# Two fused attention layers on one core: the first two pairs' row maxima from fp32 products, their sums copied by engines, a new list of steps

## The chip, the cores and the metric

One Trainium2 chip, one of its cores. The metric is the device time of one execution in microseconds (us): 652.89 us, the median of three runs (650.82 to 654.00). TensorE (PE) multiplies, VectorE (DVE), ScalarE (ACT) and GpSimd (POOL) do the rest, and SyncE (SP) issues the DMAs.

## The reference

A causal attention with a decaying bias, and behind it, on its output, a mixture of four attention heads. Batch 8, 576 positions.

```
# first layer: 8 heads of 64 columns
scores = scale * q @ k.T                      # causal
cum    = cumsum(max(s, 0))
scores = scores + min(-(cum[i] - cum[j]), 0)
attn   = softmax(scores);  x = attn @ v       # joined to [B, 576, 512]
# second layer: 4 experts of 64 columns, each with its own wq, wk, wv, wo
logits = x @ w_gate;  the 2 largest of 4, softmax over them = w
out   += w[e] * (softmax(causal(scale * (x wq[e]) (x wk[e]).T)) (x wv[e])) wo[e]
```

A softmax subtracts each row's maximum first. The kernel computes the causal bias as cum[j] - cum[i]; the second term is the same for a whole row and drops out, so a score is q·k plus the running sum at the key.

## The kernel before, in words

**Pairs and slots.** The work is cut into 48 pairs: two heads (or experts) of one batch, with the two heads side by side on the partitions. Pairs 0, 1, 2, ... are numbered in order, four first-layer pairs of a batch and then two second-layer pairs of the batch before it. A list written out by hand, `ORDER`, gives every step of the kernel as "slot:step"; the engines take their instructions from it in this order, each its own in its own queue, and wait on semaphores where a step needs another's result. Nothing else plans. Slot n holds the scores of pair n, the product with V of pair n-1, the maxima m3 to m5 of pair n+1 and m0 to m2 of pair n+2, the minus-maximum of pair n+1 and the preparation of later pairs. Slots -2 and -1 come before the first scores; so "-1:m3" is of pair 0 and "0:m3" of pair 1.

**A pair.** The scores stand keys by queries in PSUM, so that their exp goes into the product with V without a transpose. Because the maximum of a query's row then lies across partitions, it is found first from a second set of products, queries by keys: six PSUM banks (m0 to m5, `MBANKS`), 2,880 columns of each head, the left head on partitions 0 to 63 and the right one on 64 to 127, in bf16 (the upper half of each fp32 word, L729). VectorE reduces each bank with the mask to a column of `mcol` (M0 to M5, L744). TensorE turns mcol round (mt, L764), ScalarE copies it negated to 9 partitions (mA, L768) and two DMAs bring it into row 96 of the queries (mq, L773), where a row of ones on the key side adds it in the score products. Then s0 to s6 (products), E0 to E6 (exp, L819), b0 to b4 (causal selects on GpSimd), d0 to d5 (sums for the denominators, GpSimd), v0 to v8 (product with V), V0 and V1.

**Two kinds of pair.** Ordinary pairs hold q and k split into a high and a low fp32r part (h and l steps) and take two products for each score (L798, L803). Pairs 0 and 1 (`DIRECT`) are loaded into one tile, `plain`, as they are (h0 queries, h1 keys), and their scores are plain fp32 products (L792). Memsets fill rows 64 to 127 (z0 and z1 on VectorE, z2 and z3 on GpSimd).

**The running sum.** s is loaded (c0), made positive and scaled (c1, ScalarE), scanned (c2, VectorE, L457), and split into three parts by cuts and subtractions (c3, c4) in buffer `PB[1]`. For pairs 0 and 1 DMAs take the rest and the high part from there into rows 64 and 65 of the keys (hc, L632); for the others the three parts go to a DRAM tile `cum` (cu, L480) and from there to the keys (hc, L663).

**Fillers.** 60 spare products of 512 bf16 columns on a tile of zeros (i0 to i59, L1381) give TensorE something to do before the first scores: 40 ahead of the first maxima, 20 behind mt of pair 0. Eight PSUM banks are taken and given back in the list's order.

Of the kernel before, what the change touches and what calls it, by code (L numbers as in the profile page):

```python
# [8 lines left out]
F32 = mybir.dt.float32  # L9
F32R = mybir.dt.float32r  # L10
BF16 = mybir.dt.bfloat16
# [28 lines left out]
def pieces(kt, q0, q1):  # L40
# [22 lines left out]

ORDER = (
# [260 lines left out]
def order(pairs):  # L325
    for x in ORDER.split():
        n, step = x.split(":")
        yield int(n), step

COPY_Q, COPY_K = 3, 9
DIRECT = (0, 1)
SPARE = 60

FB = [0, 8, 10, 12]
NQK1 = 2
NQK2 = 3
RC = 96
RM = 96
# [1145 lines left out]
```

## Time and profile before

| | |
|---|---|
| median of three runs | 652.89 us |
| the profiled execution's own time | 653.66 us |
| its span, first to last instruction | 651.9 us |
| mean granted clock of TensorE, of 1.00 | 0.988 |
| TensorE busy | 639.9 us, 98% |
| VectorE, ScalarE, GpSimd busy | 514.0, 467.4, 414.4 us |

The span is 1.76 us shorter than the execution's time, which the profile doesn't show inside. TensorE's busy time is modelled (a product counts until its result is out, and products overlap), so 98% is not 98% of its peak. The granted clock is 1.00 at 2.4 GHz and 0.50 at 1.2 GHz.

### The profile page before, as it was taken

Reading aid. Unit: us, or ns where it says so; the run is one execution under the profiler, and the core shown is the slowest. Engines: PE = TensorE matmul, PEld = TensorE weight load, DVE = VectorE, ACT = ScalarE, POOL = GpSimd, SP = SyncE. Lnnn points to the kernel's source line nnn. Section 1 sums busy time; section 2 is a strip of 40 time slices with the busy share of each in tenths; the row PEclk is TensorE's granted clock in tenths of the full one; section 3 lists DMA queues with packets and bytes.
Section 4 is the critical chain, followed back from the end, with each engine's and each line's share of the span. In section 5 each row is a group of like instructions: output and inputs, shape, how many; then the busy total and the mean of one; then the engine's idle time right before and its main releaser. Section 6 shows DMA issues by size and latency. Waiting matters only on the chain.

```text
span 651.9 us, 16521 instructions
## 1 busy us (share of the span) xinstructions
PE 639.9 (98%) x5891; PEld 529.3 (81%) x5891; DVE 514.0 (79%) x1459; ACT 467.4 (72%) x1077; POOL 414.4 (64%) x558
## 2 busy tenths in 40 slices
PE   7999999999999999999999999999999999999997
PEld 3377798888887898888888888878987888889875
DVE  7587978996888768988778788888778867874894
ACT  5268978777768767777677767777587866576564
POOL 9298567676756585675594758638765669837030
PEclk9699999999999999999999999999999999999999
DMA  7433553452547446264464346553445725232313
GB/s 169 138 111 102 154 144 103 134 136 62 148 112 182 104 129 170 72 179 140 125 170 136 120 95 166 146 145 109 112 129 157 203 61 129 59 110 73 95 45 114
DMA packets 49559, 81.29 MB, mean 125 GB/s; under 512 B 19892, under 2 KB 19892, under 8 KB 49478
## 3 DMA queue, kind: packets, MB, share of 16 engines
q1 hardware_dynamic: 49478, 80.24, 46.4%
q8 instruction: 47, 0.77, 0.5%
q14 instruction: 34, 0.28, 0.1%
HBM read 44.61 MB, written 10.16 MB: 84 GB/s over the span
## 4 chain that ended last, share of the span: by engine, by line
PE 92%; DMA 3%; ACT 2%; DVE 1%; SPq 1%; issue 1%; ACTq 0%; DVEq 0%
PE pvp L908 20%; PE pq L1138 16%; PE s L798 11%; PE s L803 10%; PE mx L730 10%; PE pw L1138 9%; PE po L1138 7%; PE sm L961 4%; DMA raw<-in_qk_dram 2%; PE s L792 2%; PE i L1381 1%; PE s L839 1%; PE po L1112 1%; PE mt L764 1%; ACT p L819 1%
## 5 line engine op out<-in xcount | busy, mean ns | idle before, releaser
L744 DVE CUSTOM_DVE_ANT_0 sink<-mx,mask 128x64 bf16<-128x64 f32 (+7 forms) x432 | 169.5, 428 | 56.2 <-PE mx L730 41.4
L819 ACT ACTIVATE p<-s 128x512 f32<-128x512 f32 x288 | 160.4, 593 | 52.1 <-PE s L803 40.0
L851 POOL TENSOR_SCALAR_AFFINE_SELECT p<-p 128x256 f32<-128x256 f32 (+1 forms) x192 | 95.4, 506 | 142.0 <-ACT p L819 117.0
L798 PE MATMUL s<-q,k 128*128 128x320 f32 (+2 forms) x552 | 149.7, 297 | 0.0
L803 PE MATMUL s<-q,k 97*128 97x320 f32 (+2 forms) x552 | 141.4, 290 | 1.3 <-DMA q<-mr 1.3
L872 POOL TENSOR_TENSOR r<-r,p 128x640 f32<-128x640 f32 (+1 forms) x92 | 128.6, 1399 | 4.3
L798 PEld LDWEIGHTS s<-q,k 128*128 128x128 f32 x552 | 105.0, 190 | 7.8 <-issue 4.0
L803 PEld LDWEIGHTS s<-q,k 97*128 97x128 f32 x552 | 105.0, 190 | 2.2 <-DMA q<-mr 1.5
L1138 PE MATMUL pq<-x,wqkh 128*128 128x288 f32 x512 | 106.2, 300 | 0.0
L908 PE MATMUL pvp<-p,v 128*64 128x128 f32 (+3 forms) x1024 | 99.9, 321 | 0.0
L705 DVE TENSOR_TENSOR q<-raw,q 64x576 fp32r<-64x576 f32 x92 | 78.7, 870 | 25.2 <-ACT q L670 9.0
L711 DVE TENSOR_TENSOR k<-raw,k 64x1024 fp32r<-64x1024 f32 (+1 forms) x92 | 82.7, 913 | 13.7 <-PE s L798 6.0
L730 PE MATMUL mx<-k,q 96*64 96x512 bf16 (+7 forms) x920 | 86.3, 293 | 1.0 <-ACT p L844 1.0
L1138 PEld LDWEIGHTS pq<-x,wqkh 128*128 128x128 f32 x512 | 81.5, 188 | 2.5 <-ACT pv L922 1.0
L908 PEld LDWEIGHTS pvp<-p,v 128*64 128x64 f32 x1024 | 63.7, 136 | 23.3 <-issue 3.0
L1138 PE MATMUL pq<-x,wqkl 128*128 128x288 f32 x256 | 75.5, 295 | 0.0
L670 ACT ACTIVATE q<-raw 64x576 fp32r<-64x576 f32 x92 | 62.0, 678 | 6.3 <-DMA raw<-in_qk_dram 5.1
L674 ACT ACTIVATE k<-raw 64x128 fp32r<-64x128 f32 (+1 forms) x92 | 61.8, 680 | 5.2 <-DMA raw<-in_qk_dram 3.1
L730 PEld LDWEIGHTS <-q 96*64 96x64 bf16 x920 | 45.0, 110 | 19.7 <-issue 6.2
L867 POOL TENSOR_TENSOR r<-p 128x256 f32<-128x256 f32 x46 | 37.4, 812 | 34.1 <-ACT p L819 34.1
L869 POOL TENSOR_TENSOR r<-p 128x384 f32<-128x384 f32 x46 | 49.2, 1070 | 11.3 <-ACT p L819 11.2
L922 ACT ACTIVATE pv<-pvp 128x256 f32<-128x256 f32 (+1 forms) x92 | 36.5, 402 | 25.4 <-PE pvp L908 25.1
(146 smaller groups left out, 1162.8 us busy)
## 6 DMA issues: line engine op xcount, KB each, us to landing
raw<-in_qk_dram SPq DMA_DIRECT2D x30, 576.0 KB
rb<-rr SPq DMA_DIRECT2D x92, 144.0 KB
q<-q SPq DMA_DIRECT2D x45, 288.0 KB
k<-k SPq DMA_DIRECT2D x39, 288.0 KB
v<-in_vm_dram SPq DMA_DIRECT2D x32, 256.0 KB
out_dram<-o SPq DMA_DIRECT2D x32, 256.0 KB
q<-mr SPq DMA_DIRECT2D x92, 2.2 KB
plain<-in_qk_dram SPq DMA_DIRECT2D x4, 288.0 KB
```

Of the source, the lines that this page charges most:

```text
L670: nc.scalar.activation(q2[0:64, j], get_raw(n)[0:64, j], AF.Copy)
L705: nc.vector.tensor_tensor(a[64:128, j], get_raw(n)[0:64, j], q2[0:64, j].bitcast(F32), op=OP.subtract)
L711: nc.vector.tensor_tensor(part(c[0:64]), get_raw(n)[64:128, :, k], part(c[64:128]).bitcast(F32), op=OP.subtract)
L730: nc.tensor.matmul(t[64 * j : 64 * j + 64, c0 : c0 + k1 - k0], q2[0:RC, 64 * qt : 64 * qt + 64], keys(n, RC, j, k0, k1).bitcast(BF16)[:, 1 ...
L744: nc.vector.tensor_tensor_reduce(sink[:, c0 : c0 + w], t[:, c0 : c0 + w], mask[:, m0 : m0 + w], scale=1.0, scalar=mcol[n][:, 9:10] if bi = ...
L798: nc.tensor.matmul(t[0:nk, c0 : c0 + q1 - q0], K1[r1(n)][:, span(j, k0, k0 + nk)], Q1[r1(n)][:, j, q0:q1], start=True, stop=False,)
L803: nc.tensor.matmul(t[0:nk, c0 : c0 + q1 - q0], K2[r2(n)][0 : RM + 1, span(j, k0, k0 + nk)], Q2[r2(n)][0 : RM + 1, j, q0:q1], start=False, ...
L819: nc.scalar.activation(ptile[n][:, x % 2, 512 * ci : 512 * ci + 512], tl[x], AF.Exp, scale=0.125)
L851: nc.gpsimd.affine_select(out=a if kt else running()[:, :, 0:128], in_=a, pattern=[[64 if kt == 4 else 0, 2], [1, nk]], compare_op=OP.is_g ...
L872: add(r[:, :, q0:S], r[:, :, q0:S], p[:, :, 1024 + c : 1024 + c + S - q0], op=OP.add)
L908: nc.tensor.matmul(cur[h][64 * j : 64 * j + 64, q0 - PVC[h] : q1 - PVC[h]], vsl(j, kt), rtile[n][:, j, 0:128] if own else ptile[n][:, j, c ...
L1138: nc.tensor.matmul(t[0:nk, 0:w], l, r, start=(x == 0), stop=(x == len(terms) - 1))
```

## The change

For pairs 0 and 1 alone: (a) the products for the maxima are fp32, over all 128 rows, where they were bf16 over 96; (b) one row of keys carries the unsplit running sum, where two rows carried two parts of it; the scan now stands on partitions 64 to 127, and pair 0's two rows are copied by ScalarE (ha) and VectorE (hb), pair 1's are brought by two DMAs; (c) the split (c3, c4) and cu no longer stand ahead of these pairs; (d) the row of maxima is made by nine fp32 products, a column of mcol (128 rows by 1) with the identity, into three PSUM tiles of one partition (mt0: query tiles 0 to 3, mt1: 4 to 6, mt2: 7 and 8), and ScalarE writes each negated into row 96 (mA0 to mA2); the turn, the copy to 9 partitions and the two mq DMAs of these pairs go. (e) Sixteen spare products fewer: 24 ahead of the first maxima, 12 among the steps up to the first scores, 8 behind. (f) One memset of PB[1] waits for cu (lz). (g) The whole list of steps is new, to its end: of TensorE's steps about one in five keeps its successor.

In the diff below the list is cut after the steps of pair 1's scores.

```diff
+MROWS = [range(0, 4), range(4, 7), range(7, 9)]
...
 ORDER = (
+    "-2:z2 -2:i2 -2:i4 -1:z0 -1:z3 -2:id -2:f21 -2:f01 -2:i6 -2:i1 -2:i23 -2:i19 -2:i10 -2:f02 "
+    "-2:z1 -2:h1 -2:i3 -2:i18 -2:i12 -2:i7 -2:i13 -2:c0 -2:c1 -2:i0 -2:c2 -2:i5 -2:hb -2:i20 -2:ha "
+    "-2:i17 -1:z2 -2:h0 0:lv -1:ld 1:lk -2:i22 -2:i11 -2:z0 -1:z1 -2:i14 -2:i8 0:h2 0:ld 1:h1 "
+    "-2:i16 1:h2 1:h0 1:l3 2:lk -2:i15 -2:i21 -1:ha -2:i9 -2:z3 -2:m1 -2:m0 -1:m5 -2:ca -2:M1 "
+    "2:w0f -2:M0 -2:m2 -2:M2 5:w0f -1:h1 -1:m4 -2:f11 -1:m3 -1:M5 -1:mt1 1:l2 -1:mA1 -2:f20 -2:f10 "
+    "-2:i24 -2:lc -2:i25 2:w0h 2:l3 2:w0l 1:lq -2:i29 -1:mt0 -1:mA0 -2:i26 -2:i27 -2:i28 -1:M3 "
+    "-2:f22 -1:M4 -1:hb -1:h0 -1:m1 0:m5 -1:m2 0:m4 0:h3 -1:m0 1:ld 2:h2 2:h0 5:w0h 0:m3 -2:c3 "
+    "-2:c4 -2:cu 1:h3 -1:mt2 -2:i34 -2:i33 2:l0 2:lv -2:f12 -1:mA2 -2:i32 -2:i31 0:h1 2:l2 -2:i30 "
+    "-2:i35 -1:M1 0:s2 -1:M0 -1:M2 0:M5 0:s0 0:E2 0:M3 0:M4 0:E0 0:s4 0:E4 0:s5 0:E5 0:b2 0:s1 "
+    "0:b3 0:h0 1:l0 1:l1 0:s3 5:w0l -2:f00 0:E1 0:b0 0:b1 -2:i36 0:mt2 0:mA2 0:mt1 0:hc 1:m4 0:d0 "
+    "0:m0 1:s6 0:m2 0:m1 0:E3 2:l1 1:w0f 0:mA1 0:s6 1:m5 1:E6 1:m3 2:lq -2:lz -2:i39 0:E6 0:b4 "
+    "-2:i41 1:w0h -2:i38 -2:i40 -2:i37 -2:i43 -2:i42 1:M5 2:h1 1:M4 1:M3 3:w0f 3:w0h 2:ld 1:s3 "
+    "1:s5 2:hc 0:d1 0:d2 3:ld 0:d3 0:mt0 0:mA0 0:d4 0:d5 2:h3 1:E3 1:E5 1:s4 1:E4 1:b3 1:b4 1:s0 "
+    "1:b2 0:M2 0:M1 1:s2 0:M0 1:mt 1:s1 3:w0l 1:hc 1:E2 2:m5 3:m4 1:mA 1:v3 1:v5 2:m3 1:mq 1:v0 "
+    "1:m1 1:w0l 1:E1 2:M5 1:d2 1:E0 1:d1 1:b1 1:m0 1:M0 1:d3 1:d0 1:v4 1:v6 1:v1 1:v2 1:V0 1:lv "
...
-SPARE = 60
+SPARE = 44
...
-        for i in range(2):
-            for j in range(2):
-                nc.gpsimd.memset(PB[i][64 - 64 * j : 128 - 64 * j, j, PT:PCOLS], 0.0)
+        for i, j in ((0, 0), (0, 1), (1, 1)):
+            nc.gpsimd.memset(PB[i][64 - 64 * j : 128 - 64 * j, j, PT:PCOLS], 0.0)
         nc.gpsimd.memset(gwt, 0.0)
         nc.gpsimd.memset(tlt, 0.0)
         nc.gpsimd.memset(tgt, 0.0)
...
     def running_sums():
-        n = B * H
         t = {}
+        g = slice(64, P)

         def load_s():
             t["s"] = sb.tile([P, S], F32, tag="pv", name="s_t", bufs=5)
-            nc.sync.dma_start(t["s"][:n], s)
+            nc.sync.dma_start(t["s"][g], s.rearrange("(p j) s -> j p s", j=2))

         def positive():
             t["r"] = sb.tile([P, S], F32, tag="pv", name="s_r", bufs=5)
-            nc.scalar.activation(t["r"][:n], t["s"][:n], AF.Relu, scale=8.0)
+            nc.scalar.activation(t["r"][g], t["s"][g], AF.Relu, scale=8.0)

         def scan():
             t["c"] = sb.tile([P, S], F32, tag="pv", name="s_c", bufs=5)
-            r = t["r"][:n]
-            nc.vector.tensor_tensor_scan(t["c"][:n], r, r, 0.0, op0=OP.add, op1=OP.max)
+            early.append(t["c"])
+            r = t["r"][g]
+            nc.vector.tensor_tensor_scan(t["c"][g], r, r, 0.0, op0=OP.add, op1=OP.max)

         c4 = PB[1].rearrange("p a b -> p (a b)")[:, 0 : 4 * S].rearrange("p (t s) -> p t s", s=S)
-        early.append(c4)

         def cut(x, y):
             nc.vector.tensor_single_scalar(
-                y[:n].bitcast(I32), x[:n].bitcast(I32), -65536, op=OP.bitwise_and
+                y[g].bitcast(I32), x[g].bitcast(I32), -65536, op=OP.bitwise_and
             )

         def first():
             cut(t["c"], c4[:, 1])
-            nc.vector.tensor_tensor(c4[:n, 0], t["c"][:n], c4[:n, 1], op=OP.subtract)
+            nc.vector.tensor_tensor(c4[g, 0], t["c"][g], c4[g, 1], op=OP.subtract)

         def second():
             cut(c4[:, 0], c4[:, 2])
-            nc.vector.tensor_tensor(c4[:n, 3], c4[:n, 0], c4[:n, 2], op=OP.subtract)
-
-        return {"c0": load_s, "c1": positive, "c2": scan, "c3": first, "c4": second}
-
-    def keep_sums():
-        for j in range(2):
-            for k in (slice(0, 512), slice(512, S)):
-                nc.sync.dma_start(cum[:, :, span(j, k.start, k.stop)], early[0][j : B * H : 2, 1:4, k])
-
+            nc.vector.tensor_tensor(c4[g, 3], c4[g, 0], c4[g, 2], op=OP.subtract)
+
+        def keep_sums():
+            for j in range(2):
+                for k in (slice(0, 512), slice(512, S)):
+                    nc.sync.dma_start(
+                        cum[:, :, span(j, k.start, k.stop)], c4[64 + 32 * j : 96 + 32 * j, 1:4, k]
+                    )
+
+        return {"c0": load_s, "c1": positive, "c2": scan, "c3": first, "c4": second, "cu": keep_sums}

     def weights(name):
         w, hi, lo, n = {
...

-        def sums_in():
-            for j in range(2):
-                hd = 2 * i + j
-                nc.sync.dma_start(whole(n)[64:66, 2 + j], early[0][hd : hd + 1, 0:2])
-
-        items["hc"] = sums_in
+        def sums_in(j):
+            c = early[0][64 + 32 * j + n : 65 + 32 * j + n]
+            d = whole(n)[64:65, 2 + j]
+            if n:
+                nc.sync.dma_start(d, c)
+            elif j:
+                nc.vector.tensor_tensor(d, c, c, op=OP.max)
+            else:
+                nc.scalar.activation(d, c, AF.Copy)
+
+        items["ha"] = lambda: sums_in(0)
+        items["hb"] = lambda: sums_in(1)
         items["h0"] = lambda: nc.sync.dma_start(whole(n)[0:64, 0:2], heads[0:64])
         items["h1"] = lambda: nc.sync.dma_start(whole(n)[0:64, 2:4], heads[64:128])
         items["z0"] = lambda: nc.vector.memset(whole(n)[64:96, 0:2], 1.0)
...
         def sums_in():
-            if n < 2:
-                for j in range(2):
-                    hd = 2 * i + j
-                    for k in (slice(0, 512), slice(512, S)):
-                        nc.sync.dma_start(
-                            k2[64:67, span(j, k.start, k.stop)].bitcast(F32),
-                            early[0][hd : hd + 1, :, k],
-                        )
-            elif ph == 1:
+            if ph == 1:
                 nc.sync.dma_start(k2[64:67].bitcast(F32), cum[b * NP1 + i])
             else:
                 nc.sync.dma_start(k2[64:67].bitcast(F32), k2[67:70].bitcast(F32))
...
             mbank[n, bi] = t = take(f"mx{n}_{bi}")
             for qt, k0, k1, c0, _ in MBANKS[bi]:
                 for j in range(2):
-                    q2 = queries(n)[:, j].bitcast(BF16)[:, 1::2]
+                    if n in DIRECT:
+                        q, k = queries(n)[:, j], keys(n, P, j, k0, k1)
+                    else:
+                        q = queries(n)[0:RC, j].bitcast(BF16)[:, 1::2]
+                        k = keys(n, RC, j, k0, k1).bitcast(BF16)[:, 1::2]
                     nc.tensor.matmul(
-                        t[64 * j : 64 * j + 64, c0 : c0 + k1 - k0],
-                        q2[0:RC, 64 * qt : 64 * qt + 64],
-                        keys(n, RC, j, k0, k1).bitcast(BF16)[:, 1::2],
+                        t[64 * j : 64 * j + 64, c0 : c0 + k1 - k0], q[:, 64 * qt : 64 * qt + 64], k,
                         start=True, stop=True,
                     )

...
         t = {}
+
+        def row(x):
+            t[x] = take(f"mt{n}_{x}")
+            for y, qt in enumerate(MROWS[x]):
+                nc.tensor.matmul(
+                    t[x][0:1, 128 * y : 128 * y + 128], mcol[n][:, qt : qt + 1], ident,
+                    start=True, stop=True,
+                )
+
+        def copy_row(x):
+            a, w = MROWS[x][0], len(MROWS[x])
+            nc.scalar.activation(
+                queries(n)[RM : RM + 1].rearrange("p j (t c) -> p t j c", c=64)[:, a : a + w],
+                t[x][0:1, 0 : 128 * w].rearrange("p (t j c) -> p t j c", j=2, c=64),
+                AF.Copy, scale=-1.0,
+            )
+            give(t[x])
+
+        if n in DIRECT:
+            items = {}
+            for x in range(3):
+                items[f"mt{x}"] = lambda x=x: row(x)
+                items[f"mA{x}"] = lambda x=x: copy_row(x)
+            return items

         def turn():
             t[0] = take(f"mt{n}")
...
             steps.update(running_sums())
-            steps["cu"] = keep_sums
             steps["id"] = lambda: make_identity(nc, ident)
             steps["ca"] = causal
             steps["lc"] = late_constants
+            steps["lz"] = lambda: nc.gpsimd.memset(PB[1][64:128, 0, PT:PCOLS], 0.0)
             for i in range(NQK2):
                 for x, f in enumerate(fill(i)):
                     steps[f"f{i}{x}"] = f
```

## Rows read from the trace of the kernel before

**Rows 1.** Part 1 of the page: busy time of each engine over the span, its share, and instructions.

```profile
PE 639.9 (98%) x5891; PEld 529.3 (81%) x5891; DVE 514.0 (79%) x1459; ACT 467.4 (72%) x1077; POOL 414.4 (64%) x558
```

**Rows 2.** Busy time by stretch (us): PE, PE's weight loads, DVE, ACT, POOL, each with its number of instructions, then the granted TensorE clock, the DMA share and GB/s.

```profile
0.00:30.00 30.00, 24.62 (x102) 9.65 (x103) 18.23 (x39) 11.53 (x17) 18.58 (x37) 0.77 0.63 167
...
30.00:60.00 30.00, 28.69 (x255) 21.73 (x255) 26.03 (x90) 21.74 (x48) 24.62 (x32) 1.00 0.31 92
...
60.00:350.00 290.00, 290.00 (x2804) 245.59 (x2804) 235.68 (x679) 222.85 (x518) 196.09 (x255) 1.00 0.52 135
...
350.00:625.00 275.00, 273.98 (x2582) 235.94 (x2579) 216.39 (x624) 199.05 (x466) 171.98 (x227) 1.00 0.44 117
```

**Rows 3.** The chain of waits over the first 60 us: start, length, what.

```profile
16.33 3.05 PE mx L730 x22
...
25.01 5.00 PE i L1381 x13
...
30.00 5.49 PE s L792 x24
...
35.49 0.11 PE mt L764
...
54.33 3.92 DMA q<-mr
```

**Rows 4.** TensorE's spare products in order of time (start, length, line, tile, shape, count).

```profile
1.35 10.72 PE L1381 MATMUL i<-sink 128*128 128x512 bf16 x40 [1.35 <-DVE sink L373]
...
20.48 9.52 PE L1381 MATMUL i<-sink 128*128 128x512 bf16 x20
```

**Rows 5.** VectorE in order of time, first 46 us: a memset of the score operands, the running sum, one cut and one subtraction of it, and the first and the last reduction of a pair's maxima.

```profile
1.59 1.02 DVE L638 MEMSET plain<- 32x1152 f32 x1 [0.30 <-issue]
...
7.32 1.35 DVE L457 TENSOR_TENSOR_SCAN s_c<-s_r 64x576 f32<-64x576 f32 x1 [2.21 <-ACT s_r L452]
...
8.70 1.05 DVE L463 TENSOR_SCALAR p<-s_c 64x576 int32<-64x576 int32 x1
...
9.78 0.75 DVE L469 TENSOR_TENSOR p<-s_c,p 64x576 f32<-64x576 f32 x1
...
30.04 0.63 DVE L744 CUSTOM_DVE_ANT_0 sink<-mx,mask 128x448 bf16<-128x448 f32 x1 [4.72 <-PE i L1381]
...
34.38 0.08 DVE L744 DVE_READ_ACCUMULATOR2_ANT mcol<- 128x1 f32 x1
```

**Rows 6.** ScalarE in order of time, first 46 us; in brackets the idle time before and what ended it.

```profile
6.60 0.68 ACT L452 ACTIVATE s_r<-s_t 64x576 f32<-64x576 f32 x1
...
7.88 1.25 ACT L698 ACTIVATE k<-raw 64x1024 fp32r<-64x1024 f32 x2
...
12.26 0.31 ACT L674 ACTIVATE k<-raw 64x128 fp32r<-64x128 f32 x1 [3.13 <-DMA raw<-in_qk_dram]
...
31.03 0.60 ACT L819 ACTIVATE p<-s 128x512 f32<-128x512 f32 x1 [7.82 <-PE s L792]
...
38.10 0.38 ACT L922 ACTIVATE pv<-pvp 128x256 f32<-128x256 f32 x1 [1.37 <-PE pvp L908]
```

**Rows 7.** GpSimd in order of time, first 46 us: the causal mask (a memset, two selects) and the first select on a pair's exponentials.

```profile
9.49 0.77 POOL L376 MEMSET mask<- 128x576 bf16 x1
...
10.34 1.08 POOL L379 TENSOR_SCALAR_AFFINE_SELECT mask<-mask 64x64 bf16<-64x64 bf16 x2
...
32.63 0.77 POOL L851 TENSOR_SCALAR_AFFINE_SELECT p<-p 128x256 f32<-128x256 f32 x2 [12.53 <-ACT p L819]
```

**Rows 8.** SyncE's queue in order of time, first 46 us: start, time to issue, line, what, count.

```profile
2.62 1.26 SPq L635 DMA_DIRECT2D plain<-in_qk_dram  x2
...
14.61 2.52 SPq L480 DMA_DIRECT2D cum<-p  x4
```

**Rows 9.** DMA issues of the first 46 us: tile, source, queue, count, size.

```profile
raw<-in_qk_dram SPq DMA_DIRECT2D x5, 576.0 KB
...
plain<-in_qk_dram SPq DMA_DIRECT2D x4, 288.0 KB
...
w_qk<-in_wqk_dram SPq DMA_DIRECT2D x3, 256.0 KB
...
v<-in_vm_dram SPq DMA_DIRECT2D x3, 256.0 KB
...
s_t<-in_s_dram SPq DMA_DIRECT2D x1, 144.0 KB
```

**Rows 10.** Busy time by stretch, columns as in rows 2, around the fall and the rise of the granted clock.

```profile
5.00:10.00 5.00, 5.00 (x24) 2.23 (x23) 2.72 (x4) 3.17 (x5) 4.70 (x18) 1.00 1.04 204
...
15.00:16.00 1.00, 0.00 (x0) 0.00 (x0) 1.00 (x9) 0.99 (x2) 1.00 (x2) 0.75 0.59 194
...
29.00:30.00 1.00, 1.00 (x6) 0.33 (x4) 0.00 (x0) 0.00 (x0) 0.00 (x0) 0.93 0.48 138
```

**Rows 11.** The chain of waits over the whole span, its shares by line.

```profile
by line: PE pvp L908 19.7%; PE pq L1138 15.6%; PE s L798 10.8%; PE s L803 10.1%; PE mx L730 9.8%; PE pw L1138 8.5%; PE po L1138 6.5%; PE sm L961 3.8%; DMA raw<-in_qk_dram 1.8%; PE s L792 1.7%; PE i L1381 1.4%; PE s L839 1.3%; PE po L1112 1.
```

**Rows 12.** TensorE in order of time, 44 to 62 us: the product behind the one wait of this stretch.

```profile
58.30 0.42 PE L803 MATMUL s<-q,k 97*128 97x320 f32 x1 [1.31 <-DMA q<-mr]
```

**Rows 13.** TensorE's waits from 60 to 625 us, all of them: who waited, for what, us in total, times, the longest.

```profile
PE mx L730 <- ACT p L844: 1.0, 1, 1.0
```

497 rows, old and new, of the table ORDER are left out of this document.

## The prediction

> **What bounds the kernel now.** I read the page's busy shares first, then the stretches, then the chain of waits for the start, then each engine's own order there. TensorE is busy 98% of the span, VectorE 79%, ScalarE 72% [rows 1]. From 60 to 625 us TensorE is busy in every microsecond but one, at a granted clock of 1.00 [rows 2], and that one is its only wait there, 1.0 us [rows 13]. So in this stretch the time is TensorE's work, and no order of steps shortens it by more than that microsecond. What can move lies ahead of 60 us.
>
> The first 30 us hold little work. 40 spare products run from 1.35 us for 10.72 us, then come the maxima of pairs 0 and 1 in bf16, then 20 more spare products from 20.48 us for 9.52 us [rows 4], and the first score product at 30.00 us [rows 3]. The clock falls at about 15.5 us, in a microsecond in which TensorE does nothing, and is back in the microsecond before the first scores [rows 10]; the mean of the 30 us is 0.77 [rows 2]. From 30 to 60 us TensorE loses 1.31 us [rows 2], all in one wait for a maxima row of a later pair, whose DMA took 3.92 us [rows 3, 12].
>
> **The maxima's cost.** The trace has no fp32 product for maxima, so it is bounded. Below: as now; 22 of the 40 products for two pairs took 3.05 us at half clock [rows 3], so 20 at full clock take 1.4 us. Above: the fp32 score products of pair 0, 24 records for 12 products and 3,072 columns, took 5.49 us [rows 3], 1.79 ns a column; 5,760 columns would take 10.3 us. Nearest is the product with V, fp32 like them, with two heads in the two halves of the columns: 19.7% of 651.9 us [rows 11] for 48 pairs is 2.68 us a pair, for 1,600 columns of each head. That is half the price of the score products, so the two halves run side by side, and 2,880 columns take 4.8 us. I take 4.8.
>
> **The products with the identity.** 128 columns at 1.79 ns are 0.23 us; nine make 2.1 us a pair. Below, as today's turn, 0.11 us in all [rows 3].
> This price is where a page speaks against the change: the Trainium skill, "TensorE: Matmul & The Clock Gate", Terms, has trn2's transpose mode four times faster for fp32. The row's 0.11 us times four would be 0.44 us a product, by estimate 4.0 us a pair in place of 2.1; my time would rise by 3.8 us. No run here shows it.
>
> **The start, step by step.**
> - s: today 576 KB go ahead of it [rows 9] and its relu starts at 6.60 us [rows 6]. Now 288 KB of keys do; 288 KB less at 204 GB/s [rows 10] is 1.4 us, so 5.2 us. Relu 0.68 [rows 6], scan 1.35 [rows 5]: 7.25 us. The copy on VectorE is priced as a subtraction of that width, 0.75, the memset behind it 1.02 [rows 5]: 9.0 us. GpSimd needs seven memsets of that size and the identity first, to about 8.9 us. TensorE's 24 spare products, at 10.72/40 us each [rows 4], end at 7.8 us. First product at 9.1 us.
> - Pair 0: 4.8 us, to 13.9. The causal mask on GpSimd, 0.77 and 1.08 us [rows 7], stands behind that last memset, so VectorE reduces from 10.8 us; six banks take 4.4 us [rows 5], and what mt1 needs is there at 13.2. mt1 0.7, three spare products at 0.21 (24 in 5 us [rows 10]), mt0 0.9, three more: 16.8 us.
> - Pair 1's last load. Ahead of it and with it go four loads of `plain` and s, two raw, one of v and two of weights, 3.25 MB [rows 9]. Today ScalarE gets the raw of pair 2 at 12.26 us [rows 6], with 2.16 MB issued up to it; the other 1.09 MB at 204 GB/s take 5.3 us: 17.6 us. TensorE waits 0.8 us. Pair 1's products end at 22.4, mt2 at 22.9. ScalarE's copy of two query tiles costs 0.38, as a copy of 256 columns [rows 6], beside six spare products, 1.25 us. First score at 24.1 us, not 30.0: 5.9 us earlier.
> - The steps taken out on SyncE's queue (mq, and the hc DMAs) free it; cu, 2.52 us of issue [rows 8], moves behind c4. On VectorE c3 and c4, two of 1.05 and two of 0.75 us at most [rows 5], move behind pair 0's reductions. The last two of these stand behind preparations: ScalarE has the raw of pair 3 at 12.3 us (again 2.16 MB issued up to it), 3.7 us of copies on it (one of keys is 1.25 us for its two parts [rows 6]), a row copy and a weight copy to 17.0; then VectorE takes the weights' low part, 0.75, and the two reductions, 1.5: 19.2 us. Behind c3 and c4 wait pair 1's reductions, whose first freed bank the third score chunk needs: 19.2 + 3.6 + two preparations of 0.75 + 0.8 is 25.1 us, against 25.9 when TensorE comes to it. That cover is 0.8 us thick. Pair 2's maxima need cu and then hc: 22.8 + 2.52 + two landings, about 29 us, against 31 when they are due.
> - Added behind the first score: eight spare products, 1.7 us; pair 1's nine products with the identity, 2.1; less two turns, 0.2. Scores and the rest are as today. 3.6 us of the 5.9 are given back: 2.3 us left.
> - The row copies, up to 0.60 us for 512 columns [rows 6], are off the path: they lie beside spare products or scores.
>
> **From there to 60 us.** exp starts 5.9 us earlier, and with it GpSimd, whose first select now comes at 32.63 us after 12.53 us idle [rows 7]. The maxima row that comes late at 58.30 us hangs on this chain, so I take its 1.31 us as gone. If it stays, that is the second rival.
>
> **The rest.** After 60 us I take nothing: bounds -1.0 (the one wait goes) and +3 (a few new waits of the kind at 58.30 us). Sum: 2.3 + 1.3 = 3.6 us. 653.66 - 3.6 = 650.1 us against the profiled execution; the median lies 0.77 us below that execution, so 649.3 us.
>
> **The rivals.**
> 1. The clock (slower). If it falls during the fp32 maxima and stays at 0.50 as long as today, 13.5 us (15.5 to 29), TensorE does 6.75 us of work less in that time, and unlike today that is real work. 649.3 + 6.75 = 656. Place: from 9 to 24 us; it decides if the waits at 7.8 to 9.1 and 16.8 to 17.6 us grow to the 1.86 us that TensorE stood still before 16.33 us today. For it: today's fall, and sixteen fillers fewer. Against: between the two waits it would be busy without a break, which today it was not. Chance 0.14.
>  The same page of the Trainium skill, Part 1: The HAM clock gate, has the half clock as the default and activity as what releases it; the trace agrees (it falls in the idle microsecond and is back at 0.93 in the last one of the second row of spare products, by rows 4 and 10).
> 2. The start's gain is given back by 60 us: VectorE is busy 26.0 of the 30 us from 30 to 60, more than its share later [rows 2], and pairs 2 to 4 may wait for their rows as pair 3 does today. What is left is 0 to 1.5 us: 651.4 to 653. Chance 0.23.
> 3. The new list makes TensorE wait anew in the steady part, three waits like that of 58.30 us: +4, 653.3 us. For it: most neighbours are new. Against: TensorE has other work in its queue at each. Chance 0.06.
> 4. The change does not do what it says: the two halves do not run side by side in fp32 here. 10.3 in place of 4.8 us, twice: +11, 660 us. Against it is the product with V. Chance 0.03.
> 5. More than forecast: loads land earlier, fp32 maxima start at 8 us, and the steady wait goes: 646. Chance 0.12.
>
> **How the numbers follow.** The forecast, 648 to 651.4 us, has 0.42. What a measurement can tell from no change is 0.5%, 3.26 us, so the bounds are 649.6 and 656.2. Faster: 0.12 and, as 649.3 lies at the edge, 0.26 of the 0.42, in all 0.38. Slower: 0.07 (half of rival 1), 0.03 and 0.02 of rival 3: 0.12. The rest, 0.50, is same. Range 645.5 to 655.5: it leaves out rival 4, half of rival 1 and the far part of rivals 3 and 5.
>
> **What would show it.** Right: first fp32 maxima at 8.5 to 10 us; a pair's six banks on TensorE in about 5 us; nine products with the identity at 0.2 us each; the granted clock at 1.00 from 5 us on; the first score at 24 us; pair 1's scores done some 2 us before today's; no wait at 50 to 60 us; 60 to 625 us as dense as now. Wrong: 0.50 in any microsecond between 9 and 30; ten microseconds for a pair's maxima; a first score after 27 us; more than 2 us of waits after 60 us.

## The result, and the profile after

The changed kernel takes 660.95 us, the median of four runs (659.58 to 663.51), the kernel before 652.42 us beside it: a ratio of 1.0136 (95% interval 1.0110 to 1.0161), 8.5 us slower. The forecast was 649.3 us, the range 645.5 to 655.5: wrong, and on the wrong side. The profiled execution, the slowest of the four, took 663.51 us, with a span of 661.8 us, 9.9 us more than the 651.9 of before.

The chain of waits of the changed kernel from 0 to 62 us (start, length, what), cut after the first scores, which answers to [rows 3]:

```profile
1.65 8.64 DMA s_t<-in_s_dram
10.32 0.69 ACT s_r L454
11.03 1.36 DVE s_c L460
12.47 2.21 DMA plain<-s_c
14.68 0.15 issue
14.82 6.64 PE mx L735 x40
21.47 0.75 PE mt L768 x6
22.22 0.75 PE i L1408 x3
22.97 0.96 PE mt L768 x8
23.93 0.76 PE i L1408 x3
24.69 5.01 PE mx L735 x40
29.70 0.53 PE mt L768 x4
30.23 0.34 PE i L1408
30.61 0.39 PE i L1408
31.04 1.02 PE i L1408 x4
32.06 5.29 PE s L819 x24
```

The first line is the news. The load of s, 144 KB, is issued nearly first and takes 8.64 us; before, with 576 KB ahead of it, its relu (the step that makes s positive) started at 6.60 us [rows 6]. Everything up to the first product hangs on it. ScalarE's own lines up to the relu, VectorE's memset behind the scan and the copy of pair 0's sums, and TensorE's lines of pair 0's maxima and first scores (start, length; in brackets the idle time before and what ended it):

```profile
0.81 1.28 ACT L454 ACT_TABLE_LOAD   x1 [0.81 <-PEq L1500]
10.32 0.68 ACT L454 ACTIVATE s_r<-s_t 64x576 f32<-64x576 f32 x1 [8.23 <-DMA s_t<-in_s_dram]
```
```profile
13.44 1.02 DVE L646 MEMSET plain<- 32x1152 f32 x1 [0.19 <-issue]
```
```profile
14.82 6.64 PE L735 MATMUL mx<-plain 128*64 128x384 f32 x40 [6.65 <-DMA plain<-s_c]
31.90 5.45 PE L819 MATMUL s<-plain 128*128 128x320 f32 x24
```

The chain and TensorE's line put the wait's end down to a DMA of `plain`, which is pair 1's row. More likely it is the memset, which ends at 14.46 us: in the three kernels `after`, `a_two` and `a_first` pair 0's products start 0.36 us behind the end of that memset (14.82, 11.53 and 12.91 us), while the trace names three different releasers. By either way they hang on the scan, and so on s.

TensorE stands still for 6.65 us, and the clock falls under it. Windows of one microsecond (from:to, then busy of PE, PEld, DVE, ACT, POOL, the granted clock, DMA share, GB/s):

```profile
10.00:11.00 1.00, 0.00 (x0) 0.00 (x0) 0.00 (x0) 0.68 (x1) 1.00 (x2) 1.00 0.90 331
11.00:12.00 1.00, 0.00 (x0) 0.00 (x0) 0.97 (x1) 0.00 (x0) 1.00 (x2) 0.60 0.15 55
...
17.00:18.00 1.00, 1.00 (x4) 0.26 (x2) 0.73 (x4) 0.99 (x2) 0.73 (x1) 0.50 1.12 207
18.00:19.00 1.00, 1.00 (x18) 0.71 (x16) 0.62 (x3) 0.64 (x2) 0.00 (x0) 0.99 0.93 183
```

So pair 0's products run at 1.2 GHz up to 18 us and take 6.64 us; pair 1's, the same forty records at 2.4 GHz, take 5.01. The later stretches, as in [rows 2], and TensorE's waits from 60 to 625 us (total, times, longest), against 1.0 us in [rows 13]:

```profile
30.00:60.00 30.00, 29.83 (x237) 20.62 (x236) 22.07 (x80) 20.32 (x43) 22.08 (x31) 1.00 0.41 114
60.00:350.00 290.00, 288.70 (x2806) 245.65 (x2803) 234.76 (x679) 224.61 (x514) 200.81 (x256) 1.00 0.50 133
350.00:625.00 275.00, 273.05 (x2561) 230.95 (x2560) 213.77 (x611) 195.38 (x460) 173.14 (x226) 1.00 0.45 119
```
```profile
PE s L830 <- DMA q<-mr: 1.9, 2, 1.3
PE s L825 <- ACT pv L949: 0.4, 1, 0.4
PE pvp L935 <- POOL r L892: 0.4, 1, 0.4
PE pq L1165 <- DVE x L1067: 0.2, 1, 0.2
```

How far the changed kernel lies behind at four points of the two traces (first scores are given here and below by TensorE's own line, where that of before starts at 29.89; the chain of [rows 3] has 30.00):

| | before | after | behind by |
|---|---|---|---|
| first score product | 29.89 | 31.90 | 2.0 us |
| turn of pair 2's maxima | 41.92 | 47.68 | 5.8 us |
| turn of the last pair's maxima | 615.25 | 624.05 | 8.8 us |
| end of the span | 651.9 | 661.8 | 9.9 us |

Over half of the loss is there by 48 us; the steady part adds 3.0, of which 1.9 is waits (2.9 against 1.0), and the end 1.1. The split between these last two is rough: a pair's turn stands at another place in the new list, and from pair to pair the turns of the changed kernel lie 3.6 to 10.6 us behind those of before.

### The profile page after: what moved, and what is told of

Same layout as the page of the kernel before. It is cut to its first block, busy times and chain, and to the rows that moved or that the text cites. A ratio compares the mean times of both kernels' runs of the same rounds, so it can differ in the third digit from the quotient of the medians.

```text
span 661.8 us, 16686 instructions
## 1 busy us (share of the span) xinstructions
PE 645.9 (98%) x5949; PEld 532.2 (80%) x5949; DVE 511.6 (77%) x1460; ACT 472.2 (71%) x1082; POOL 418.2 (63%) x558
## 4 chain that ended last, share of the span: by engine, by line
PE 90%; DMA 5%; DVE 2%; SPq 1%; ACT 1%; issue 1%; POOL 0%; ACTq 0%; DVEq 0%
PE pvp L935 19%; PE pq L1165 15%; PE s L825 11%; PE mx L735 11%; PE s L830 10%; PE pw L1165 8%; PE po L1165 6%; PE sm L988 4%; PE s L819 2%; DMA s_t<-in_s_dram 1%; PE s L866 1%; DMA q<-q 1%; PE po L1139 1%; PE mt L791 1%; PE i L1408 1%; DVE sink L747 1%
## 5 line engine op out<-in xcount | busy, mean ns | idle before, releaser
L878 POOL TENSOR_SCALAR_AFFINE_SELECT p<-p 128x256 f32<-128x256 f32 (+1 forms) x192 | 93.4, 495 | 149.5 <-ACT p L846 137.3
L825 PE MATMUL s<-q,k 128*128 128x192 f32 (+2 forms) x552 | 151.3, 299 | 0.7 <-ACT pv L949 0.4
L830 PE MATMUL s<-q,k 97*128 97x192 f32 (+2 forms) x552 | 141.5, 291 | 1.9 <-DMA q<-mr 1.9
L899 POOL TENSOR_TENSOR r<-r,p 128x640 f32<-128x640 f32 x92 | 130.0, 1413 | 5.3
L712 DVE TENSOR_TENSOR k<-raw,k 64x1024 fp32r<-64x1024 f32 (+1 forms) x92 | 81.3, 894 | 15.9 <-DMA k<-k 9.7
L735 PE MATMUL mx<-k,q 96*64 96x256 bf16 (+7 forms) x920 | 87.9, 293 | 0.0
L896 POOL TENSOR_TENSOR r<-p 128x384 f32<-128x384 f32 x46 | 52.0, 1131 | 12.4 <-ACT p L846 12.4
L1054 DVE TENSOR_TENSOR pv<-pv,rb 128x576 f32<-128x576 f32 x46 | 43.5, 948 | 10.3 <-DMA rb<-rr 9.7
```

What stands on the lines that cost most here:

```text
L712: nc.vector.tensor_tensor(part(c[0:64]), get_raw(n)[64:128, :, k], part(c[64:128]).bitcast(F32), op=OP.subtract)
L735: nc.tensor.matmul(t[64 * j : 64 * j + 64, c0 : c0 + k1 - k0], q[:, 64 * qt : 64 * qt + 64], k, start=True, stop=True,)
L825: nc.tensor.matmul(t[0:nk, c0 : c0 + q1 - q0], K1[r1(n)][:, span(j, k0, k0 + nk)], Q1[r1(n)][:, j, q0:q1], start=True, stop=False,)
L830: nc.tensor.matmul(t[0:nk, c0 : c0 + q1 - q0], K2[r2(n)][0 : RM + 1, span(j, k0, k0 + nk)], Q2[r2(n)][0 : RM + 1, j, q0:q1], start=False, ...
L878: nc.gpsimd.affine_select(out=a if kt else running()[:, :, 0:128], in_=a, pattern=[[64 if kt == 4 else 0, 2], [1, nk]], compare_op=OP.is_g ...
L899: add(r[:, :, q0:S], r[:, :, q0:S], p[:, :, 1024 + c : 1024 + c + S - q0], op=OP.add)
```

## The experiments

Unless said otherwise, a time is a median beside runs of the kernel before on the same chip (651.5 to 652.0 us), and a first score is that of the profiled execution.

**The load of s.** In the changed kernel one DMA reads s as two halves of 32 rows, `(p j) s -> j p s`, so that its first dimension counts 2. In `a_two` the same bytes go to the same partitions in two DMAs of 32 rows:

```diff
-            nc.sync.dma_start(t["s"][g], s.rearrange("(p j) s -> j p s", j=2))
+            for j in range(2):
+                nc.sync.dma_start(
+                    t["s"][64 + 32 * j : 96 + 32 * j], s.rearrange("(p j) s -> j p s", j=2)[j]
+                )
```

> The changed kernel, s loaded by two DMAs of 32 rows each in place of one with two dimensions. Theory A (the one load of s is slow by its form, two outer entries that only few DMA engines serve): relu of s begins at 5.0 to 6.6 us in place of 10.32, the first maxima product at 9 to 11 us in place of 14.82, the clock stays at 1.00, the first score at about 26 us; the time falls by 5 to 7 us, to about 655 us. Theory B (s is late because v and two raw loads issued behind it share the engines): relu still at 9 to 10.5 us, the time within 1 us of the changed kernel.

656.75 us, ratio 1.0082 (1.0045 to 1.0120). In its trace:

```profile
5.73 1.28 ACT L457 ACT_TABLE_LOAD   x1 [5.73 <-DMA s_t<-in_s_dram]
7.03 0.68 ACT L457 ACTIVATE s_r<-s_t 64x576 f32<-64x576 f32 x1
```
```profile
11.53 5.08 PE L738 MATMUL mx<-plain 128*64 128x384 f32 x40 [2.18 <-DMA raw<-in_qk_dram]
27.05 5.45 PE L822 MATMUL s<-plain 128*128 128x320 f32 x24
```

The relu is 3.3 us earlier, TensorE waits 2.18 us in place of 6.65, the clock stays at 1.00, the products take 5.08 us and the first score comes 4.85 us earlier: 4.2 us of the 8.5 are gone. The load itself gains more than the relu does. By the semaphore records of the traces s has landed at 5.66 us, 4.6 us earlier; the relu then waits for ScalarE's `ACT_TABLE_LOAD` of 1.28 us, which stands behind the wait for s here, and in the changed kernel ran at 0.81 us, long before s. All eight kernels here with s in two DMAs have it there, at 5.40 to 5.73 us; no run moves it, and what it costs in the end was not tried.

`a_first` leaves the load as the change has it and puts the DMA of pair 1's first row (`-1:ha`), which waits for the scan, ahead of the loads of v and raw on SyncE's queue:

```diff
-... -2:h0 0:lv -1:ld ... 2:lk -2:i15 -2:i21 -1:ha
+... -2:h0 -1:ha 0:lv -1:ld ... 2:lk -2:i15 -2:i21
```

> The changed kernel with its one load of s; the DMA of pair 1's first row of sums stands in SyncE's queue right behind the load of pair 0's queries, so that v and both raw loads are issued only after the scan. Theory A: with the engines to itself the load still needs several us on few engines, relu at 7 to 9 us. Theory B: relu at 5 to 6 us. The time by either is unsure by 3 us, since the raw loads now come later; the relu's start is what tells.

662.12 us, 1.0161 (1.0139 to 1.0184). The relu starts at 8.34 us: with little behind it in the queues the load is 2.0 us quicker, and still its landing is 2.7 us later than that of the two loads of `a_two` with all the others behind them (8.32 against 5.66). What was held back lands late, so that pair 1's maxima and the first score (33.6 us) come later.

`b_form` puts the form of the load alone into the kernel before (the rows are picked accordingly behind it):

```diff
-            nc.sync.dma_start(t["s"][:n], s)
+            nc.sync.dma_start(t["s"][:n], s.rearrange("(p j) s -> j p s", j=2))
```

> The kernel before, with the changed kernel's form of the load of s (one DMA, two outer dimensions, heads in the order even then odd; the rows are picked accordingly behind it). Theory A: relu at 9.5 to 12 us in place of 6.60, the first maxima 3 to 5 us later; the time rises by 2 to 5 us since twenty spare products behind the maxima hide nothing of it. Theory B: relu at 6.6 us as before, same time.

657.0 us, 1.0076 (1.0048 to 1.0104), and in its trace

```profile
11.32 0.69 ACT s_r L452
...
32.80 5.49 PE s L793 x24
```

the relu is 4.7 us later than in [rows 6] and the first score 2.8 us later than before. By the medians the access pattern costs 4.2 us in one kernel and 5.1 in the other. The 5.1 holds more than the load: the profiled execution is the fastest of `b_form`'s four (654.69 us, span 1.1 us longer than before), and the other three, 656.8 to 658.8 us, ran at a lower mean clock (0.985 to 0.987 against its 0.989). That `a_first`'s load was 2.0 us quicker says that loads issued behind it slow it too; it holds them back in turn: of pair 0's queries, issued behind it, 14 of the sixteen increments of the semaphore have come by 7.06 us in the changed kernel, the last two at 10.09 and 10.88, where in `a_two` all have come by 7.10.

**The fp32 maxima.** `b_fp32` is the kernel before with fp32 products for pairs 0 and 1 (two memsets moved forward for it), nothing else; `a_two_bf16` is `a_two` with bf16 ones.

```diff
-                    q2 = queries(n)[:, j].bitcast(BF16)[:, 1::2]
+                    if n in DIRECT:
+                        q, k = queries(n)[:, j], keys(n, P, j, k0, k1)
```

> The kernel before with the maxima of pairs 0 and 1 as fp32 products over 128 rows and nothing else of the change (two memsets of the score operands stand earlier, so that all rows are filled). At 5.0 us a pair at full clock in place of 1.3 to 1.5 the first score comes 4 to 7 us later if the clock stays up, 10 or more if it falls as it does before; the time rises by that much. If the wait for the maxima row, and not TensorE, held the first scores, the time rises by under 2 us.

652.88 us, 1.0016 (0.9995 to 1.0038): no difference. Ten microseconds of products (12.65 to 22.9) stand where the idle time and half-clock fillers were, and the clock stays up:

```profile
0.00:30.00 30.00, 27.31 (x142) 13.41 (x143) 18.13 (x40) 11.55 (x17) 18.29 (x37) 1.00 0.57 143
```

against 24.62 us at 0.77 in [rows 2]. The price of the products and the clock that they keep up cancel here. One of the 23 runs of the kernel before beside `b_fp32` kept its clock by itself: mean 1.000, a span of 644.5 us, where the median is 650.2 and `b_fp32` has 649.6 to 651.6 at 0.999 to 1.000. There is no trace of that run, but by it fp32 maxima do cost some 6 us at the same clock.

> As the first of these runs (s in two DMAs), and the maxima of pairs 0 and 1 from bf16 products again, 96 rows, on the one row of sums. The maxima are then rounded, which a softmax cancels. If fp32 products cost what the page's shares gave (4.8 us a pair against 1.4), this is faster than the first run by up to 6.8 us less what pair 1's loads then leave waiting: first score at 22 to 24 us, 3 to 6 us faster. If the loads of pair 1 bind instead of the products, the gain is under 2 us.

655.22 us, 1.0051 (1.0031 to 1.0071): first score at 23.4 us, 3.6 us ahead of `a_two`, with 1.5 us of it left in the time. So what the fp32 products cost net is small, and not the cause. Net, since the clock goes the other way again: in the profiled execution of `a_two_bf16` the first 30 us have a mean clock of 0.89, in that of `a_two` 1.00.

**The new list.** `b_rest` keeps the kernel before up to pair 1's scores and then follows the new order; `h_two` and `h_two_bf16` take the start of `a_two` and then the order of before; `a_two_36` leaves out the eight spare products behind the first score.

```diff
-    ORDER of before, to its end
+    ORDER of before up to 1:s4, then what is left in the new ORDER's sequence
```

> The kernel before to the end of pair 1's scores, and from there the steps in the changed kernel's order; nothing else of the change. Theory C (the new list itself costs time behind the start: the runs so far are 3 to 5 us longer than their start explains): 654 to 656 us, 2 to 4 us slower than before. Theory D (the list is as good, the rest is in the start): within 1 us of before.

659.93 us, 1.0119 (1.0073 to 1.0165), 5 us lost at the seam by pair 3 (waits of 1.7 us for v, 1.6 and 1.0 for GpSimd's sums): two halves of different lists don't fit at such a seam, and it says little of the list itself.

> The changed kernel with s in two DMAs to the end of pair 1's scores (first score at 27.1 us, pair 1's scores done 0.9 us later than before by the same row), and from there the steps in the order of the kernel before. Theory C: 2 to 4 us faster than with the new list, 652.5 to 654.5 us. Theory D: 656 to 657 us as with the new list.

658.81 us, 1.0111 (1.0070 to 1.0152).

> As the run before it, with the maxima of pairs 0 and 1 in bf16 on the one row of sums. Theory C: the start's gain of some 2 us is kept, 649 to 651 us, faster than the kernel before. Theory D: 654 to 655.5 us, as with the new list.

654.11 us, 1.0039 (1.0016 to 1.0062). Old order behind the new start: 2.1 us worse than the new one in fp32, 1.1 us better in bf16, on other chips than `a_two` and `a_two_bf16` and with intervals that overlap. Neither order is clearly the worse one.

> The changed kernel with s in two DMAs and without the eight spare products behind the first score (36 in place of 44), same list otherwise. If TensorE's work behind the first score counts in full, as the prediction had it, the run is 1.7 us faster than with them (656.75 us): 655 us. If the time there is held by another engine or by a landing, the difference is under 0.5 us.

655.93 us, 1.0063 (1.0045 to 1.0081); the intervals of this and of `a_two` overlap. The run doesn't decide between its two cases: in its profiled execution the clock fell under pair 0's maxima (6.69 us for the forty products in place of 5.08), and the first score came at 28.44 us, later than in `a_two`.

**Three that were meant to win.** `best_mix` takes `a_two`, issues the memsets early, drops eight spare products, has bf16 maxima for pair 1, puts pair 0's scores ahead of pair 1's maxima, moves pair 3's preparations behind them and then follows the list of before; `best_bf16` is the same with bf16 for both, `best_mix_new` with the new list.

```diff
-    ... -1:mA0 (pair 1's maxima) ... -1:mt2 -1:mA2 0:s2 0:s0 0:s4 0:s5 0:s1 0:s3
+    ... -1:mA0 -1:mt2 -1:mA2 0:s2 0:s0 0:s4 0:s5 0:s1 0:s3 (preparations of pair 3, pair 1's maxima)
```

> s in two DMAs; both memsets of pair 0's and 1's query rows ahead of the scan; pair 0's maxima fp32, pair 1's bf16; pair 0's last two reductions and its row of maxima ahead of ScalarE's and VectorE's preparations for pair 3; pair 0's scores ahead of pair 1's maxima; no spare products behind the first score; from the end of pair 1's scores on the order of the kernel before. First maxima product at 9.5 to 10.5 us, first score at 17 to 19 us (27.1 us with s in two DMAs alone). If TensorE's work holds the time from there, pair 1's scores end 4 to 6 us earlier than before and the time is 646 to 649 us. If the loads or the other engines hold it, the gain is used up by 60 us: 650.5 to 652.5 us.

> As the run before it, with pair 0's maxima in bf16 too. Its products take 1.4 us in place of 5.0 but VectorE's six reductions, 4.4 us, follow them, so the first score comes at most 1 us earlier; the clock may fall to 0.50 between 10 and 20 us, which fp32 products prevent, and then it comes 2 us later. Time within 1.5 us of that run.

> As best_mix up to the end of pair 1's scores, and from there the changed kernel's order of steps. It tells the two lists apart once more behind one and the same start: by theory C 2 to 4 us slower than best_mix, by theory D within 1 us of it.

662.41 us (1.0162, 1.0143 to 1.0182), 664.39 (1.0199, 1.0180 to 1.0219) and 662.34 (1.0172, 1.0151 to 1.0192). Misses all three, and this is why, in `best_mix`:

```profile
20.25 5.45 PE L821 MATMUL s<-plain 128*128 128x320 f32 x24 [0.50 <-ACT plain L777]
25.53 0.81 PE L1410 MATMUL i<-sink 128*128 128x512 bf16 x3
26.27 1.49 PE L737 MATMUL mx<-plain 96*64 96x384 bf16 x20
27.69 1.47 PE L1410 MATMUL i<-sink 128*128 128x512 bf16 x6
38.97 2.57 PE L770 MATMUL mt<-ident,mcol 128*1 128x128 f32 x10 [9.81 <-DVE mcol L749]
```

The first score comes at 20.25 us, and then TensorE stands 9.81 us for pair 1's column of maxima: on VectorE its reductions stood in the queue behind subtractions of pair 3 and the cuts of the sums, which waited for ScalarE's copies up to 31 us. An early score is worth nothing when the next one's work is queued behind something late. `best_mix` and `best_mix_new` agree (662.41 and 662.34 us): behind this start, the lists make no difference in the time.

**The first score by itself.** What then is an earlier first score worth? Three kernels move it in the kernel before (with the fp32 maxima of `b_fp32`) and keep loads, copies and later steps in the order that they had in their queues. `c_few` drops 8 of the 20 spare products ahead of it. `c_turn` turns pair 0's row and sends it off before pair 1's maxima, which then cover the two DMAs, so that 14 spare products can go. `c_turn_16` has these 14 back. In `c_turn` SyncE sends pair 0's row at 20.41 us in place of 24.42 (`b_fp32`), so the loads queued behind it start 4.0 us earlier too; `c_turn_16` has the same early loads, and so these two differ by the first score alone.

```diff
-... -1:m3 ... 0:m5 0:m3 0:m4 -1:m0 -1:m1 ... -1:m2 -1:M5 -1:M3 -1:m4 -1:M4 -1:mt (20 spares with -1:mA, -1:mq) 0:s5
+... -1:m3 -1:m4 ... -1:M5 -1:M3 -1:M4 (4 spares) -1:mt -1:mA -1:mq 0:m5 0:m3 0:m4 -1:m0 -1:m1 -1:m2 (2 spares) 0:s5
```

> The kernel before with fp32 maxima (as b_fp32), and one thing moved: pair 0's row of maxima is turned and sent off before pair 1's maxima, which then cover its DMAs, so 14 of the 20 spare products behind the turn go. No load, no copy and nothing after the first scores is moved. Theory 'carried': the first 30 us of the kernel before are TensorE's spare products, so an earlier first score (25 us in place of 30) reaches the end: 647 to 648.5 us. Theory 'given back': what pairs 1 to 4 wait for (VectorE's and ScalarE's preparations, the loads) doesn't start earlier, so by 60 us TensorE waits for it and the end is where it was: 651 to 653 us.

> The kernel before with fp32 maxima (as b_fp32) less the last 8 of the 20 spare products between the turn and the first score, 8 x 0.25 us. 'Carried': first score at 28 us, 650.5 to 651 us in the end. 'Given back': 652 to 653, as b_fp32.

> c_turn with 14 of the spare products put back, behind pair 1's maxima. 'Carried': first score 14 x 0.25 = 3.5 us later than in c_turn and the end as much later. 'Given back': the same end as c_turn, within 1 us.

`c_turn` takes 648.24 us, ratio 0.9933 (0.9909 to 0.9958): faster than both kernels of this case. `c_few` 650.03 (0.9969, 0.9950 to 0.9989), `c_turn_16` 651.10 (0.9981, 0.9958 to 1.0004). "Carried" holds in all three. From `c_turn`:

```profile
12.99 5.08 PE L733 MATMUL mx<-plain 128*64 128x448 f32 x40
18.94 1.04 PE L1382 MATMUL i<-sink 128*128 128x512 bf16 x4 [0.86 <-DVE mcol L745]
19.81 0.27 PE L765 MATMUL mt<-ident,mcol 128*9 128x128 f32 x1
20.01 5.08 PE L733 MATMUL mx<-plain 128*64 128x256 f32 x40
25.03 0.61 PE L1382 MATMUL i<-sink 128*128 128x512 bf16 x2
25.48 5.63 PE L793 MATMUL s<-plain 128*128 128x320 f32 x24
```
The first score products of `c_few` and of `c_turn_16`:

```profile
28.04 5.63 PE L794 MATMUL s<-plain 128*128 128x320 f32 x24
```
```profile
28.44 5.63 PE L795 MATMUL s<-plain 128*128 128x320 f32 x24
```

`c_turn` from 30 to 350 us, as in [rows 2]:

```profile
30.00:60.00 30.00, 30.00 (x314) 23.33 (x312) 25.38 (x87) 25.05 (x57) 29.23 (x39) 1.00 0.43 119
60.00:350.00 290.00, 290.00 (x2792) 245.64 (x2789) 237.98 (x688) 221.09 (x512) 196.07 (x253) 1.00 0.51 133
```

First score at 25.48 us, 4.4 us before that of before; pair 2's turn is 4.4 us ahead of before, the wait of [rows 12] is gone too (5.9 us ahead at pair 4), and at the last pair it is still 4.7 us. Between `c_turn` and `c_turn_16` the first score moves 2.96 us (25.48 to 28.44) and the time 2.86 us. `c_few` gains more than it moved: its first score is 1.74 us ahead of `b_fp32`'s (29.78) and its time 2.85 us less, on another chip; `b_fp32`'s profiled execution loses clock late (last section), that of `c_few` does not.

## Why the prediction was wrong

**The step that failed: "s: ... Now 288 KB of keys do; 288 KB less at 204 GB/s is 1.4 us, so 5.2 us."** The relu started at 10.32 us. The step reckoned by the bytes queued ahead and did not look at the form of the load itself. Half of the loss comes from that (4.2 of 8.5 us, `a_two`), and `b_form` shows it apart from everything else.

Its sum by bytes was nearly right for the form of before. The load landed at 6.58 us there, by the trace's semaphore records, so 6.60 was a landing; in `a_two`, with that form in two DMAs and 288 KB less ahead, it lands at 5.66, 0.9 us earlier where the step had 1.4. The relu starts at 7.03 us even so, since the `ACT_TABLE_LOAD` stands between, which the forecast did not have.

Page and trace: the Trainium skill, "DMA: Bandwidth & Descriptors", Why a DMA increments its semaphore by 16 and not by 1, has a DMA shared out over the largest number of engines, up to 16, that divides the slowest dimension of both its sides; by that rule a first dimension of 2 gives two engines, one of 32 sixteen. The traces agree (8.64 us, against 4.0 us from the first issue to the landing of two loads of 32 rows), and so does the count of increments of the load's semaphore: in the changed kernel one at 2.71 us and then two, at 9.42 and 10.30; in the kernel before sixteen, from 5.14 to 6.58 us, and in `a_two` sixteen for each of its two DMAs, from 4.37 to 5.66. The diff had this line in plain sight.

**The clock (rival 1).** Its place and condition were right: "if the waits ... grow to the 1.86 us that TensorE stood still before". The wait grew to 6.65 us, the clock fell at 11 us and was back at 18. Its price was 6.75 us in the forecast; it measured 1.6 us (6.64 less 5.01), as most of the half-clock time was waiting, and it is a result of the late s, not a cause of its own.

The first score, forecast for 24.1, came at 31.9. Of these 7.8 us, 5.1 are s; 0.6 lie from relu to first product, in the gaps between the steps that the sum set end to end (4.50 us in place of 3.9; the last gap, from the memset to the product, is 0.36); 1.8 are pair 0's products; 0.2 the rest. That rest, 10.4 us from the end of pair 0's maxima to the first score, was forecast as 10.2.

**What was right.** Two halves in fp32 side by side: 5.0 us a pair against 4.8, so rival 4 is dead. Products with the identity at 0.25 us each (eight records, four products, in 1.0 us on the chain above) against 0.23. "3.6 of the 5.9 are given back behind the first score": measured 3.8 (5.8 less 2.0), and in `a_two` the first score is 2.8 us early and pair 2's turn 0.9 late, 3.7. The wait at 58.3 us is gone. That what is left of an earlier first score reaches the end was right as well, by `c_turn`; but with s as in `a_two` there is nothing left to carry, 2.8 us less 3.7: of the 3.0 us by which its first score misses the forecast (27.05 against 24.1), the relu at 7.03 and not 5.2 took 1.8.
The Trainium skill, "TensorE: Matmul & The Clock Gate", Terms, by which the forecast weighed an estimate of 0.44 us for such a product, is not borne out as a price ratio here: 0.25 us against the turn's 0.11.

**After 60 us.** Taken as nothing, with a bound of +3: measured +3.0 to the last pair's turn and 1.1 behind it, with the reserve on turns said above. New waits are 1.9 of it, 1.3 at once for a maxima row. That is rival 3's place at half its price.

`a_two` is 4.8 us slower than before in the median although its pair 2 is only 0.9 late. Its trace splits this: behind before by 0.9 at pair 2's turn, 1.8 at the last pair's and 4.5 at the end (span 656.4 against 651.9). So the steady part is not where it goes. Of the 2.7 behind the last turn, 1.7 are a fall of the clock at 631 us (last section), which neither the trace of before nor that of the changed kernel has. The other 1.0 stands in the traces with the new list (1.1 in the changed kernel, 1.0 in `a_two_bf16` and `best_mix_new`) and not in those with the old one (0.0 in `c_turn` and `h_two_bf16`). Whether it is time lost or only the place of the turn in the list stays open, and with it whether the new list costs anything: `best_mix` and `best_mix_new` take the same time, and in `h_two` against `a_two` the old order is 2.1 us the slower.

## What to carry to other kernels

When a diff rewrites the access pattern of a load that heads the chain, price that pattern before the bytes: look at its first dimension. A consumer's start isn't always a landing: in `a_two` s is there at 5.66 us, and the relu starts at 7.03, behind a table load. Where the start is fillers and TensorE is the bound behind it, a microsecond won at the first real product is a microsecond at the end, provided that what it starts isn't queued behind something late; order the work so that real products cover a DMA's latency, as `c_turn` does, instead of buying that cover with spare ones.

## What the runs showed of the hardware

One load of 144 KB took 8.64 us in one form, and in another it had landed 4.0 us after its issue (1.66 to 5.66 us); the slow one ends in two late increments of its semaphore, the quick ones in sixteen each. Ten microseconds of fp32 products left the time of `b_fp32` as it was, with the granted clock of the first 30 us at 1.00 where it had been 0.77. An `ACT_TABLE_LOAD` of ScalarE takes 1.28 us and can come to stand behind a wait for data: it ran at 0.81 us in some kernels and at 5.73 in `a_two`.

The clock also falls late in the kernel, where TensorE's rows show no wait, in some executions and not in others: in 6 of the 17 profiled ones it does so some 20 us before the end. The five runs of `a_two` have spans of 652.5, 653.5, 655.0, 656.4 and 659.5 us at mean clocks of 1.000, 0.999, 0.997, 0.997 and 0.991: its spread goes with the clock. The one at the full clock took 2.3 us more than the median span of before beside it (650.2 us), whose clock of 0.988 to 0.992 has the fall of its first 30 us in it. Near the end of its profiled execution (656.4 us; windows of 2 us):

```profile
630.00:632.00 2.00, 2.00 (x13) 1.08 (x14) 0.94 (x2) 1.93 (x8) 0.87 (x3) 0.85 0.25 94
632.00:634.00 2.00, 2.00 (x14) 1.40 (x12) 1.64 (x3) 0.11 (x1) 1.82 (x4) 0.50 0.93 255
634.00:636.00 2.00, 2.00 (x20) 1.33 (x18) 0.39 (x1) 0.72 (x2) 0.00 (x0) 0.80 0.14 48
```

TensorE is busy throughout, and by the three windows the lower clock costs 1.7 us of its work at full clock (0.15, 0.50 and 0.20 of 2 us each). In the first 30 us, with the same start, `h_two` waited 2.98 us where `a_two` waited 2.18, the clock fell, and its forty products took 6.76 us in place of 5.08.
